# Sparse attention into a routed mixture of experts: routing and constants issued in pieces, a shorter tile list, half weight loads, expert units placed anew, and output scaling on ACT

## The chip, the cores and the metric

One core of a Trainium2 chip runs the whole program. The metric is the device time of one execution in microseconds (us), which is the span from the first to the last instruction plus 1.6 to 2.1 us. Timings came from several chips, numbered in the runs. Every comparison is made on one chip, or names the chips.

Engines: PE is TensorE, PEld its weight loads, DVE is VectorE, ACT is ScalarE, POOL is GpSimd, SP is SyncE.

## The reference, cut to what matters

```python
# B, H, S, D = 4, 8, 768, 64; block, window = 32, 16;  N, DM, E, F = 3072, 512, 8, 1024
k_sum = k.reshape(B, H, nb, block, D).max(axis=3)
v_sum = v.reshape(B, H, nb, block, D).mean(axis=3)
scores = concat(where(|i - j| < window, q k / 8, -1e9), q k_sum / 8 + log(block))
attn = softmax(scores) @ concat(v, v_sum)
x = attn.transpose(0, 2, 1, 3).reshape(N, DM)

logits = x @ w_gate + modality_bias[modality_id]      # 8 experts, one per token
e_idx, gate = argmax(logits), softmax(logits)[e_idx]
out[mask_e] = gate * (relu(x[mask_e] @ w1[e]) @ w2[e])
```

## The kernel before

The kernel runs attention in 16 **steps**, one for each batch and pair of heads. Behind every fourth step a batch is complete and is **routed**: logits, one-hot, the place of each token in its expert's region of a DRAM buffer `xs`, six indirect DMAs of 128 rows that **scatter** the tokens there, and the **tile list**, which says which expert tiles (256 tokens of one expert) are now full. A tile's rows then come back as `xr`, are transposed (`px`), and go through w1, ReLU and w2. An expert tile is cut into **units** (a `yield` each, one group of eight matmuls), and the table `UNITS` says how many of them each attention step carries. TensorE takes its matmuls in program order, so where a unit is placed decides what stands behind it.

What the change touches (cut):

```python
    def later_constants():                 # one block, at the end of step 0
        nc.vector.tensor_scalar(erev, cidx[:, 0:E], -1.0, float(E), op0=ALU.mult, op1=ALU.add)
        # ... eleven more small DVE operations ...
        for t in xrs:                      # 8 row buffers
            nc.gpsimd.memset(t, 0.0)
        # ... eight more, then
        pm = bank([128, NJ], FP16, "pm")
        nc.tensor.transpose(pm, mh, ident[0:NJ, 0:NJ])
        nc.vector.tensor_copy(midf, pm)

    # in expert_tile:
            nc.vector.tensor_scalar_mul(ot, po, gt)

    UNITS = [0] * 6 + [3] * 4 + [6] * 4 + [0, 0]

    def weights_ahead(n):                  # guessed experts' weights, 1 MB each
        when = {1: (0, 0), 2: (0, 1), 4: (1, 0), 5: (1, 1)}
        if n in when:
            u, w = when[n]
            # ... expert index from the guess ...
            load_weights(u, gv[u], which=(w,))

    for n in range(np_):
        u = [UNITS[n] * (i + 1) // 6 - UNITS[n] * i // 6 for i in range(6)]
        # load(n + 5)
        weights_ahead(n)
        scores(n, 1)
        if new and cc == 1:
            enlist(*new)                   # rows and weights of the new tiles
        if n and cc == 0:
            features(n - 1)
            router = route(b - 1)
            step(router)                   # logits to one-hot, in one go
        pump(u[0])
        # keys(n + 2); pump(u[1])
        values(n, 0)
        # summaries(n + 2)
        if router:
            step(router)                   # ranks, index, six scatters
        # pump(u[2]); queries(n + 2); pump(u[3]); blocks(n + 1); scores(n + 1, 0)
        if router:
            drain(router)                  # the tile list, some 30 DVE operations
        # pump(u[4]); features; values(n, 1)
        if n == 0:
            later_constants()
        pump(u[5])
```

The softmax here doesn't subtract the row's maximum and nothing guards it: scores larger than these inputs give would overflow.

## Time and profile before

| | kernel before |
|---|---|
| timed, first pair (4 runs) | 276.9 us (276.3 to 277.7) |
| profiled execution | 269.1 us, span 267.5 |
| busy: PE, DVE, ACT, POOL | 189.3, 161.6, 105.2, 128.1 us |
| DVE instructions | 486 |

The profiled execution is 7.5 us shorter than the timed ones. The page's rows of 40 equal slices (busy share of PE in tenths, then the TensorE clock that was granted) show the holes of the first half and the half clock that follows each:

```profile
PE   1272088693436979849999799597870998999920
PEclk9999559759555797985999889889596899999975
```

Counted from 0, a slice being 6.7 us, slices 3 and 4 are the constants' hole, 10 to 12 step 6, and 28 to 30 the last routing. The prediction shows the lines of these holes.

### The profile page before, as it was taken

How to read it: one execution, taken by the hardware profiler on the slowest of the kernel's cores; microseconds unless marked ns; L12 is line 12 of the kernel's file. 1: busy time of each engine (PE TensorE's matmuls, PEld its weight loads, DVE VectorE, ACT ScalarE, POOL GpSimd, SP SyncE). 2: the span in 40 equal slices, each digit the busy share in tenths (PEclk: the TensorE clock that was granted, in tenths of full speed). 3: DMA queues.
4: the chain of work that ended last, by engine and by line, in shares of the span. 5: the costliest groups of instructions: out<-in, count | busy, mean ns of one | idle time of the engine just before them, and what ended most of it. 6: DMA issues, size and time to landing. Idle time of an engine off the chain costs nothing. (4 is left out here: it accounts for less than half of the span.)

```text
span 267.5 us, 6780 instructions
## 1 busy us (share of the span) xinstructions
PE 189.3 (71%) x2680; PEld 133.9 (50%) x2680; DVE 161.6 (60%) x486; ACT 105.2 (39%) x185; POOL 128.1 (48%) x202
## 2 busy tenths in 40 slices
PE   1272088693436979849999799597870998999920
PEld 0162077583334756723768465375550674677600
DVE  2539969988923675998566668957659224232110
ACT  2256069566303643831548145354030321333300
POOL 7739948727606432587305046530155776422220
PEclk9999559759555797985999889889596899999975
DMA  6996099996794961139802012330022333211100
GB/s 87 190 171 92 1 170 207 207 208 163 116 222 63 144 88 45 41 121 220 195 2 82 0 59 82 98 125 0 21 100 79 83 79 157 82 78 78 76 16 0
DMA packets 20027, 27.09 MB, mean 101 GB/s; under 512 B 2812, under 2 KB 16404, under 8 KB 19988
## 3 DMA queue, kind: packets, MB, share of 16 engines
q0 software_dynamic: 17360, 24.17, 43.9%
q1 hardware_dynamic: 2628, 2.41, 3.2%
q8 instruction: 23, 0.38, 0.6%
q14 instruction: 16, 0.13, 0.2%
HBM read 85.27 MB, written 10.25 MB: 357 GB/s over the span
## 5 line engine op out<-in xcount | busy, mean ns | idle before, releaser
L515 PE MATMUL pmo<-w2b,hT 128*128 128x512 f16 x208 | 57.6, 432 | 7.6 <-DVE tk L445 7.6
L504 PE MATMUL ph<-xg,w1b 128*128 128x256 f16 x416 | 53.8, 283 | 4.6 <-DVE at L490 3.3
L521 POOL DMA_INDIRECT out_dram<-ot,at x26 | 25.8, 992 | 57.8 <-DVE ot L520 44.0
L507 ACT ACTIVATE hT<-ph 128x512 f16<-128x512 f32 x52 | 31.1, 608 | 48.8 <-PE ph L504 48.8
L504 PEld LDWEIGHTS <-w1b 128*128 128x128 f16 x416 | 39.9, 101 | 13.3 <-issue 3.7
L250 ACT ACTIVATE pT<-pss 128x384 f16<-128x384 f32 x64 | 28.1, 505 | 44.0 <-PE pss L246 43.4
L515 PEld LDWEIGHTS <-hT 128*128 128x128 f16 x208 | 21.5, 108 | 33.5 <-issue 17.6
L520 DVE TENSOR_SCALAR ot<-pmo,xr 128x512 f32<-128x512 f32 x26 | 19.3, 747 | 29.1 <-PE pmo L515 22.0
L251 DVE TENSOR_TENSOR pT<-pT,bmask 96x768 f16<-96x768 f16 x32 | 19.2, 599 | 18.9 <-ACT pT L250 18.9
L201 ACT COPY kv<-pk 128x768 f16<-128x768 f16 x32 | 24.2, 808 | 15.9 <-PE pk L200 15.9
L358 POOL DMA_INDIRECT xs<-xb,posi x24 | 24.1, 1003 | 11.6 <-issue 5.8
L224 ACT COPY qT<-pq 128x768 f16<-128x768 f16 x16 | 13.0, 812 | 17.8 <-PE pq L222 17.8
L204 POOL COPY kv<-kv 128x352 f16<-128x352 f16 x16 | 7.9, 494 | 23.3 <-ACT kv L201 23.2
L233 PE MATMUL pv<-ident,kv 128*128 128x128 f16 x192 | 16.5, 248 | 3.1 <-POOL kv L214 3.1
L272 DVE TENSOR_TENSOR xb<-po,rec 128x384 f16<-128x384 f32 x32 | 17.8, 558 | 1.2
L281 PE MATMUL pt<-ident,xb 128*128 128x128 f16 x96 | 10.1, 240 | 11.6 <-DVE xb L272 11.6
L488 DVE COPY xg<-px 128x1024 f16<-128x1024 f16 x13 | 8.9, 685 | 15.4 <-PE px L486 15.4
L246 PE MATMUL pss<-qT,kv 64*128 64x64 f16 x384 | 12.7, 205 | 5.7 <-POOL kv L214 5.5
L233 PEld LDWEIGHTS <-kv 128*128 128x128 f16 x192 | 14.0, 112 | 4.5 <-POOL kv L214 3.7
L211 DVE TENSOR_REDUCE ks<-kv 128x24 f16<-128x768 f16 x16 | 15.1, 943 | 1.1 <-ACT kv L201 1.1
L214 POOL COPY kv<-ks 128x576 f16<-128x576 f16 x16 | 10.7, 669 | 10.1 <-DVE ks L213 9.4
L234 ACT COPY vb<-pv 120x768 f16<-120x768 f16 x16 | 13.1, 818 | 5.4 <-PE pv L233 5.4
(142 smaller groups left out, 300.8 us busy)
## 6 DMA issues: line engine op xcount, KB each, us to landing
w1b<-in_moe_w_dram POOLq DMA_DIRECT2D x15, 1024.0 KB
w2b<-in_moe_w_dram POOLq DMA_DIRECT2D x15, 1024.0 KB
kn<-in_k_dram POOLq DMA_DIRECT2D x16, 192.0 KB
vn<-in_v_dram POOLq DMA_DIRECT2D x16, 192.0 KB
qn<-in_q_dram POOLq DMA_DIRECT2D x16, 192.0 KB
xr<-xs SPq DMA_DIRECT2D x8, 258.0 KB, 5.9
out_dram<-ot,at POOLq DMA_INDIRECT x26
xs<-xb,posi POOLq DMA_INDIRECT x24
```

What stands on the lines that cost most here:

```text
L201: nc.scalar.copy(kv[:, i, :, 0:64].rearrange("p t (s c) -> p t s c", c=C8), bass.AP(pk.tensor, pk.offset, [pk.ap[0], [8, NT], [1, 8], [P8, ...
L211: nc.vector.reduce_max(ks[:, 0], kv[:, 0, :, 0:64].rearrange("p t (g s) -> p t g s", g=2), axis=AX.X)
L233: nc.tensor.transpose(pv[:, tl, :], kv[:, 1, 6 * half + tl, :], ident)
L250: nc.scalar.activation(pT[:, h], pss[h], AF.Exp, scale=SCALE)
L251: nc.vector.tensor_tensor(pT[0:WK], pT[0:WK], bmask[0:WK, None, 6 * half:6 * half + 6, :].to_broadcast([WK, 2, 6, 64]), op=ALU.mult)
L272: nc.vector.tensor_tensor(xo, po[:, :, :, 0:D], rec.unsqueeze(3).to_broadcast([128, 2, 3, D]), op=ALU.mult)
L358: apart("xs", nc.gpsimd.indirect_dma_start(out=xs[:, :], out_offset=bass.IndirectOffsetOnAxis(ap=posi[:, c:c + 1], axis=0), in_=xb[:, c, : ...
L504: nc.tensor.matmul(ph[:, f, :], w1[:, c, ts(2 * f2 + f, 128)], xg[:, c, :], start=(c == 0), stop=(c == NCD - 1))
L507: nc.scalar.activation(hT[:, 2 * f2:2 * f2 + 2, :], ph, AF.Relu)
L515: nc.tensor.matmul(po, hT[:, f, ts(s2, 128)], w2[:, f, :], start=(f == 0), stop=(f == NF - 1))
L520: nc.vector.tensor_scalar_mul(ot, po, gt)
L521: apart("out", nc.gpsimd.indirect_dma_start(out=out[:, :], out_offset=bass.IndirectOffsetOnAxis(ap=at[:, s2:s2 + 1], axis=0), in_=ot[:], i ...
```

## The change

Its intent: no DVE block may stand in front of attention. The constants shrink; fourteen small ones move in front of the first step, and the rest come in pieces; routing is a generator of fifteen pieces, one `tick()` each between attention's parts; the tile list takes about half the operations; the guessed weights are loaded in halves, one per step (two in step 2), behind GpSimd's neighbour copies; units are placed by a string for each step; and ACT scales the output. The diff, cut to its core:

```diff
@@ constants
-        for t in xrs:
-            nc.gpsimd.memset(t, 0.0)
+        for t in xrs[-2:]:
+            nc.vector.memset(t, 0.0)
+        yield                               # and seven more yields between the rest
@@ routing: a yield behind every two or three operations; fused operations
-        nc.vector.tensor_scalar(can, lg, 0.0, None, op0=ALU.is_ge)
-        nc.vector.tensor_tensor(can, can, bc(erev, NC), op=ALU.mult)
+        st_(can, lg, 0.0, bc(erev, NC), op0=ALU.is_ge, op1=ALU.mult)
+        yield
@@ tile list: one selection over a table in place of counting and indexing
+        nc.vector.tensor_tensor_scan(cu, v2, v2, 0.0, op0=ALU.add, op1=ALU.bypass)
+        nc.vector.tensor_tensor(sel, bc(v2, T), bc(cidx[:, 1:T + 1], K * E, 2), op=ALU.is_equal)
+        nc.vector.tensor_tensor(pd, sel..., tab..., op=ALU.mult)
+        nc.vector.reduce_sum(lf[:, 0:T, 0:3], pd, axis=AX.X)
@@ expert_tile
-            nc.vector.tensor_scalar_mul(ot, po, gt)
+            nc.scalar.activation(ot, po, AF.Copy, scale=gt)
@@ schedule
-    UNITS = [0] * 6 + [3] * 4 + [6] * 4 + [0, 0]
+    UNITS = {6: "000011", 7: "101010", 8: "101110", 9: "101010",
+             10: "000111", 11: "111110", 12: "101110", 13: "101110", 14: "101110", 15: "101110"}
@@ weights_ahead
-        when = {1: (0, 0), 2: (0, 1), 4: (1, 0), 5: (1, 1)}
+        for p in {1: (0,), 2: (1, 2), 3: (3,), 4: (4,), 5: (5,), 6: (6,), 7: (7,)}.get(n, ()):
+            load_weights(p // 4, gv[p // 4], which=(p // 2 % 2,), part=p % 2)
@@ loop: tick() between all parts; enlist(...) at the end of each second step of a batch
```

## The prediction

> **What bounds the kernel now.** I read the page first, then a table of nine stretches, then the list of PE in order of time, and last the waits of the stretches with holes. The page gives PE 189.3 us of a 267.5 us span, so no engine is full on average, and the question is which engine is missing where. The stretches (columns: span, then busy of PE, weight loads, DVE, ACT, POOL; granted clock, DMA share, GB/s) are cut at PE's holes and at borders of loop steps:
>
> ```profile
> 0.00:15.00 15.00, 2.60 (x50) 2.04 (x52) 5.58 (x30) 3.68 (x4) 11.87 (x25) 1.00 0.95 146
> 22.50:34.50 12.00, 0.06 (x5) 0.01 (x1) 11.61 (x25) 1.74 (x4) 11.78 (x16) 0.63 0.47 53
> 34.50:69.20 34.70, 25.48 (x604) 21.81 (x606) 30.45 (x98) 23.18 (x41) 21.26 (x33) 0.75 1.03 190
> 69.20:89.00 19.80, 10.69 (x140) 7.96 (x138) 10.39 (x20) 5.30 (x9) 8.55 (x18) 0.50 0.88 141
> 89.00:122.70 33.70, 27.93 (x455) 19.05 (x454) 25.80 (x89) 17.50 (x32) 17.16 (x27) 0.85 0.44 90
> 122.70:187.60 64.90, 57.16 (x825) 37.93 (x824) 45.00 (x129) 30.45 (x56) 21.95 (x37) 0.89 0.30 82
> 187.60:206.80 19.20, 11.02 (x99) 7.65 (x100) 13.39 (x61) 2.63 (x5) 8.23 (x10) 0.77 0.19 70
> 206.80:257.60 50.80, 47.49 (x336) 31.36 (x335) 14.76 (x30) 14.33 (x24) 24.32 (x34) 0.97 0.24 85
> ```
>
> Row two is an almost dead PE. Row three (loop steps 1 to 5) is bound by DVE, 30.45 of 34.7 us. Row four is step 6, with both engines half idle. Rows five and six are near PE's bound with holes in each routing. Row seven is the last routing, row eight the remaining expert tiles, which fill PE. The holes, from PE's list in order of time:
>
> ```profile
> 34.49 0.20 PE L181 MATMUL pm<-ident,mh 24*128 24x24 f16 x1 [11.94 <-DVE mh L179]
> 68.24 0.50 PE L281 MATMUL pt<-ident,xb 128*128 128x128 f16 x3 [4.74 <-DVE xb L272]
> 77.69 1.04 PE L486 MATMUL px<-ident,xr 128*128 128x128 f16 x8 [6.59 <-DMA xr<-xs]
> 84.17 1.46 PE L233 MATMUL pv<-ident,kv 128*128 128x128 f16 x12 [2.52 <-POOL kv L214]
> 118.26 0.50 PE L281 MATMUL pt<-ident,xb 128*128 128x128 f16 x3 [3.42 <-DVE xb L272]
> 170.92 1.03 PE L504 MATMUL ph<-xg,w1b 128*128 128x256 f16 x8 [3.34 <-DVE at L490]
> ```
>
> The first is the block of constants, the second, fifth and sixth are the tile-list arithmetic (some 30 dependent DVE operations in one run) standing in front of attention's DVE work. The third and fourth come with the Pool's wait for its own weight load; the whole waits have it beside the last hole, where PE stands until the last tile list is in a register:
>
> ```profile
> POOL w2b L187 <- DMA w2b<-in_moe_w_dram: 11.1, 1, 11.1
> ...
> PE pmo L515 <- DVE tk L445: 7.6, 1, 7.6
> ```
>
> Why the constants take so long is in the lines by form: three DVE operations on 8 or 16 elements stand for 6 us each, exactly under the Pool's eight memsets.
>
> ```profile
> L169 POOL MEMSET xr<- 128x1032 f16 x8 | 7.3, 974 | 0.0
> L153 DVE TENSOR_SCALAR erev<-cidx 128x8 f32<-128x8 f32 x1 | 6.2, 6205 | 0.0
> ```
>
> **What the Trainium skill says.** (1) "SBUF — State Buffer", section "Who interferes with whom": DVE in a two-port mode and GpSimd share one port pair by an exclusive lock, and the loser fully blocks. The trace agrees: erev, an fp32 tensor_scalar, lasts 6205 ns until the memsets end, while equal small ones elsewhere last 0.16 to 0.29 us. (2) "TensorE: Matmul & The Clock Gate", Part 1: after an idle window of about 3.4 us PE runs at half clock. The trace agrees: eight w2 matmuls take 1.89 us warm and 3.55 us at 124.6, after the hole at 118. So a hole costs more than its length. (3) "ScalarE: Activation LUTs", "What ACT_TABLE_LOAD costs": 186 ns + 0.833 N with immediate scale, 93 ns more with a pointer scale. For N=512 that is 612 ns; the trace's ReLU is 608 (31.1 us in 52), so the new scaling is estimated at 0.70 us, DVE's being 0.747. (4) "DMA: Bandwidth & Descriptors", "Bandwidth": 1 MB takes 6.15 us alone. Here the last guessed load (issued 70.33, waited for until 82.41) took some 12 us, behind q, k, v and row loads. So halves issued earlier should wait far less.
>
> **The change part by part.**
>
> *Start, +1 us.* Load 1 now goes ahead of the iotas: three Pool issues, 0.63 us apart, move them 1.9 us. The mask constants' end moves from 8.7 to 10.6; early constants (14 small operations) add 1.9; two summary reductions (0.86 + 0.94) and the Pool copy (0.67) give first scores at 15.1 against 14.96. The Pool is no longer behind load issues, but DVE takes that place. Load 3 then stands before summaries 1, worth up to 1 us. No gain here.
>
> *Constants, -5.4 us.* PE's hole is 12.0, but DVE finishes step 0's work at 25.6, so only 25.6 to 34.2 is lost, 8.6. What is left as pieces: two memsets of 0.5, and about ten operations, 3.2 in all, still on the bound engine. 8.6 - 3.2 = 5.4.
>
> *Routing 0 and its list in the DVE-bound stretch, -4.2.* Before: eight operations to one-hot at about 0.22 (1.75), nine to the scatter (1.9), about thirty from cf to done (6.1), two tk (0.5): 10.2. After: eleven at 0.22 (2.5) plus sixteen at 0.2 (3.3): 6.0. A normal step's DVE work is, start to start, 2x0.48 mask, 2x0.21 reciprocal, 2x0.47 scale, 2x0.86 reductions, 0.47 vb, 0.48 xT: 5.0 us; steps 1 to 3 took 5.1 on average, so savings here shorten the span one for one. Step 6 should start at 69.2 - (5.4 + 4.2 - 1) = about 60.5.
>
> *Step 6, -8.3.* Before 19.8 with 3 expert units. The weight wait goes; tile 1's weights come at step 7, where the Pool waits for half a megabyte, an estimate of 4 to 5 us, with neighbour copies already out and two steps of slack. What stays: six scatters at 1.29 each (7.7), then the row load of about 6 to 7, against a first expert unit placed five stations into the step. From the scatters' start to rows is some 15.7 us, PE arrives 2 to 4 earlier. 5.5 attention + 2 units at 1.2 + 3.5 wait = 11.5.
>
> *Steps 7 to 15, -12.6.* Before 98.6 with 33 units. A clean step is step 11 (137.48 less 148.96): 11.48 us, PE full, 6 units. Six units cost about 7.3 (eight w1 matmuls four times 0.93, px 0.5, w2 twice 1.82, less overlap), so a unit is 1.22 and attention 4.1. After, 34 units: 34x1.22 = 41.5; attention 7x4.1 + 2.6 + 1.8 = 33.1; routing matmuls 1.6: 76.2. To this I add DVE in step 9 (5.0 + 0.4 + list 4.0 = 9.4 against PE's 7.8) 1.6, rows of list 1 about 2 and the half clock behind it 2, Pool at step 7 1, rest 3: 86. Spreading 8 units into steps 14 and 15, which had none, fills their 0.5 us holes.
>
> *Last routing and tail, -6.* The units left are 43 both times (36 of 79 done), and PE does them at 7.39 us per six in the last stretch. The last list is not shorter: before, cf to li is 6.97; after, two operations on 1440 elements (estimated 1.65 each, from 0.66 for 480) eat what the fewer operations save, and I sum to 7.0. But pr and pc matmuls no longer stand behind blocks of three units (pr waited 3.8, pc 3.5). Chain from pl: 1.9 to one-hot, 2.1 through pr to the scatter index and count, 1.3 through pc, 7.0: 12.3, beside eight units of 9.9. Hole 2.5 to 3.5 instead of 7.6, and less half clock (two stretches of eight w2 matmuls at 3.2 and 3.4 instead of 1.9): -6.
>
> Scaling on ACT is worth nothing alone: DVE loses 26x0.747 = 19.3 us where PE is the bound.
>
> Sum: -4.2 + 1 - 5.4 - 8.3 - 12.6 - 6 = -35.5 of the span. Taken off the timed run: 276.6 - 35.5 = 241.
>
> **The rivals.**
> *DMA takes over.* The stretch at 34.5 already has a DMA share of 1.03 at 190 GB/s. Without the hole, loads and half-weights come closer together: 3.7 MB in about 16 us of steps 1 to 3, 230 GB/s, above what it moved. For it: the numbers. Against: q, k, v are five steps ahead, and only one wait for kn shows, at the start. If it binds, half of the constants' and step 6's gain goes: 248.
> *The new wait on ACT.* With three ot buffers, scaling waits for the out scatter behind ten gathers; DVE waited 6.6 us for it at 216.9 and PE lost 1.25. On ACT the ReLUs stand behind it. I expect some 1 us, at most 4: 242 to 245.
> *DVE stays the bound.* If the shorter list's pieces each wait for PE or the wider operations run slower, steps 8, 9, 12, 13 keep 1.5 each: 247.
> *Everything overlaps well*: no row waits, holes closed in step 6: 232.
>
> **Range and chances.** Two thirds of the gain are closed holes that one can point at; one third is my assumption of 92% PE efficiency after step 6. If I get only half of steps 6 to 15, it is 251; if rows never wait, 232. 241, range 229 to 255. Faster by over 2% (under 271) 0.95, within 2% 0.04, slower 0.01.
>
> **What would show it.** Right: no PE hole over 4 us between 20 and 140; the small constants at 0.2 us; step 6 starting near 60; the end of attention near 158; the last hole 2 to 4 us; the Pool's longest weight wait under 6. Wrong: waits of PE for kn or vn (DMA), of hT behind ot on ACT, or PE in the middle stretch under 85% busy. A rise in slower matmuls at full occupancy would break my unit price.

## The result, and the profile after

Ratios here are the mean time of one kernel's fast runs over that of the other's fast runs of the same rounds, so not quite the ratio of the medians that are quoted. Executions over 1.5% slower than the fastest of the same kernel are left out of the means.

| first pair | before | after |
|---|---|---|
| timed, 4 runs each | 276.9 us | 268.2 us (266.3 to 270.6) |
| ratio | | 0.966 (0.960 to 0.972) |
| span of the profiled run | 267.5 | 266.6 |
| busy PE, DVE, ACT, POOL | 189.3, 161.6, 105.2, 128.1 | 193.5, 128.1, 122.4, 126.3 |
| DVE instructions | 486 | 361 |

The change is faster by 3.4%. The predicted 241 us and its range, 229 to 255, are missed by far. The page's same two rows for the changed kernel:

```profile
PE   0375966753859895597998776998973829999920
PEclk9999996555558999577999995999999965999995
```

The first 30 us are fuller than before, but there are weak slices where I had foretold none: 9 (60 to 67 us), 15 and 16 (100 to 113), 30 and 32 (200 to 207 and 213 to 220). What TensorE does there is in its list in order of time (start, duration, line, operation, then the idle time before it and what ended it), here in step 9:

```profile
104.95 0.28 PE L287 MATMUL po<-vb,pT 120*64 120x65 f16 x5 [0.50 <-issue]
105.71 0.26 PE L287 MATMUL po<-vb,pT 120*64 120x65 f16 x4 [0.49 <-issue]
106.45 0.21 PE L287 MATMUL po<-vb,pT 120*64 120x65 f16 x1 [0.48 <-issue]
...
108.62 1.01 PE L498 MATMUL ph<-xg,w1b 128*128 128x256 f16 x4 [0.45 <-issue]
...
112.25 0.24 PE L244 MATMUL pq<-ident,qn 96*64 96x96 f16 x1 [0.36 <-issue]
```

Twelve `po` matmuls, ordinarily one group of 0.36 us, are cut into **bursts** that start some 0.72 to 0.76 us apart. "issue" means that TensorE waited for nothing that the profile shows. The other engines wait for TensorE meanwhile, and the releaser is not even seen. That is how the page's group of the ReLU reads in this run, and below it the same group in the rerun that follows:

```profile
L501 ACT ACTIVATE hT<-ph 128x512 f16<-128x512 f32 x52 | 30.6, 605 | 20.3 <-remote 13.9
L501 ACT ACTIVATE hT<-ph 128x512 f16<-128x512 f32 x52 | 31.0, 603 | 9.1 <-PE ph L498 6.9
```

There are four such stretches (59.5 to 66, 104 to 113, 156 to 163, and parts of 197 to 220 us), and each lies in a row of GpSimd's indirect DMAs: three rows of six scatters, and the last routing's scatters with ten gathers behind them. Many records of semaphores are missing too: counted in the stored trace (no page shows the count), there are 2,710 records of semaphore updates.

So there are two questions. What are the bursts? And what did the change do apart from them?

### The profile page after: what moved, and what is told of

Read it like the earlier page. It is cut to its first block, busy times and chain, and to the rows that moved or that the text cites. A ratio compares the mean times of both kernels' runs of the same rounds, so it can differ in the third digit from the quotient of the medians.

```text
span 266.6 us, 6691 instructions
## 1 busy us (share of the span) xinstructions
PE 193.5 (73%) x2684; PEld 137.1 (51%) x2684; DVE 128.1 (48%) x361; ACT 122.4 (46%) x211; POOL 126.3 (47%) x198
## 5 line engine op out<-in xcount | busy, mean ns | idle before, releaser
L509 PE MATMUL pmo<-w2b,hT 128*128 128x512 f16 x208 | 53.4, 407 | 6.1 <-issue 4.2
L498 PE MATMUL ph<-xg,w1b 128*128 128x256 f16 x416 | 54.7, 283 | 3.6 <-issue 3.6
L509 PEld LDWEIGHTS <-hT 128*128 128x128 f16 x208 | 20.2, 102 | 30.7 <-issue 8.5
L514 ACT ACTIVATE ot<-pmo,xr 128x512 f32<-128x512 f32 x26 | 18.0, 692 | 28.9 <-PE pmo L509 26.2
L290 DVE RECIPROCAL rec<-po 128x6 f32<-128x6 f32 x32 | 6.0, 187 | 30.6 <-PE pq L244 13.2
L255 PE MATMUL pv<-ident,kv 128*128 128x128 f16 x192 | 18.8, 268 | 1.8 <-POOL kv L236 1.0
L287 PE MATMUL po<-vb,pT 120*64 120x65 f16 x384 | 15.3, 215 | 6.5 <-issue 2.9
L244 PE MATMUL pq<-ident,qn 96*64 96x96 f16 x256 | 13.5, 244 | 7.2 <-issue 6.3
L255 PEld LDWEIGHTS <-kv 128*128 128x128 f16 x192 | 15.8, 123 | 5.2 <-issue 2.2
L268 PE MATMUL pss<-qT,kv 64*128 64x64 f16 x384 | 13.3, 211 | 5.9 <-POOL kv L236 5.9
```

The costliest lines, as they stand in the source:

```text
L255: nc.tensor.transpose(pv[:, tl, :], kv[:, 1, 6 * half + tl, :], ident)
L287: nc.tensor.matmul(po[64 * (tl % 2):64 * (tl % 2) + 64, h, tl // 2, :], pT[0:KR, h, tl, :], vb[0:KR, 6 * half + tl, h, :])
L498: nc.tensor.matmul(ph[:, f, :], w1[:, c, ts(2 * f2 + f, 128)], xg[:, c, :], start=(c == 0), stop=(c == NCD - 1))
L509: nc.tensor.matmul(po, hT[:, f, ts(s2, 128)], w2[:, f, :], start=(f == 0), stop=(f == NF - 1))
L514: nc.scalar.activation(ot, po, AF.Copy, scale=gt)
```

## The experiments

### Is it the kernel? (both kernels once more, on chip 3)

No edit.

> The changed kernel once more, unedited. In its first trace TensorE runs four stretches (59.5-66.2, 103.7-113.0, 155.9-163 and parts of 197-220 us) in bursts of five to ten instructions about 0.72 us apart, with no wait that the profile shows, some 20 us of loss by my reading; each lies in a run of GpSimd's indirect DMAs. If this is a property of the kernel's order (theory A: the runs of indirect DMAs; theory B: a place in TensorE's own instruction stream), all four come back within 2 us of those times, and the time is 266 to 271. If it is chance, they move or vanish and the time falls below 262.

> The kernel before once more, because its first trace (267.5 us) is 8 us shorter than its timed runs (276 to 278). If the timed runs of the kernel before hold the same bursts of TensorE in some runs of indirect DMAs, this trace will be about 275 long and show gaps of 0.7 us without a shown wait, 5 to 10 us in sum, and then theory A covers both kernels. If it shows none, and is again near 268, the state of the clock alone made the difference.

Measured, one run each, so of unknown state: changed kernel **242.7** us, before 263.3 (span 261.7). The kernel before took 261.3 to 268.9 in seven further runs there. All the bursts are gone, and there are 3,263 records of updates in place of 2,710 for the same program. The expectation "all four come back" was wrong: the bursts are not in the kernel's order alone. Two of the four rows of indirect DMAs, as stretches (span; then busy time with the count of instructions of PE, PEld, DVE, ACT, POOL; clock; DMA share; GB/s). First the first trace of the changed kernel:

```profile
104.10:111.50 7.40, 3.93 (x26) 1.66 (x25) 0.41 (x2) 0.80 (x1) 5.87 (x6) 0.64 0.35 129
202.10:217.60 15.50, 8.82 (x63) 5.42 (x64) 0.76 (x2) 3.38 (x6) 12.22 (x16) 0.93 0.30 85
```

Then the same rows of DMAs in the rerun on chip 3:

```profile
98.00:105.40 7.40, 6.64 (x146) 4.67 (x143) 7.13 (x22) 5.75 (x12) 5.88 (x8) 1.00 0.38 136
184.60:200.10 15.50, 12.03 (x76) 6.96 (x74) 1.52 (x4) 4.45 (x7) 12.14 (x16) 0.89 0.35 102
```

GpSimd takes the same 5.9 us for its scatters both times and the DMA share is about the same, but TensorE gets 26 matmuls through instead of 146. The two stretches don't begin at the same matmul, so here is the same piece of work, from the first `po` to the last `pq` of step 9. It took 9.3 us in the first trace (104.24 to 113.50) and 1.8 us in the rerun, where these lines are its first and last. At half clock throughout it would be some 3.6 us, so the clock alone does not explain it:

```profile
97.45 0.36 PE L287 MATMUL po<-vb,pT 120*64 120x65 f16 x12
...
98.72 0.53 PE L244 MATMUL pq<-ident,qn 96*64 96x96 f16 x16
```

### Two kinds of chips (the changed kernel on whatever chip came)

No edit in the four anchors.

> The changed kernel unedited, timed against the kernel before on the chip of these runs. On chip 3 one look gave 242.7 against 264.7, in the first pair of timings 268.2 against 276.9. If the bursts of TensorE belong to the chip or to its state in the first pair, they show here only if both kernels are again near 268 and 277; otherwise a ratio of 0.91 to 0.92 and 241 to 245 us.

> The changed kernel unedited, as the anchor of these runs: ratio 0.91 to 0.92 to the kernel before on a chip that runs that in 262 to 266. If the chip is one that runs the kernel before in 276 to 278, the bursts of TensorE are expected again, at 59-66, 104-113, 156-163 and 197-220 us, and 266 to 271 us.

> The changed kernel unedited as the anchor: 241 to 245 with 3,260 to 3,280 records of semaphore updates on a chip that runs the kernel before in 262 to 266; 266 to 271 with bursts and some 2,700 records of updates on a chip that runs it in 276 to 278. A chip of the second kind has to show both together, or my tie between them is wrong.

> The changed kernel unedited once more, for another chip. 239 to 245, some 3,270 records of semaphore updates and no bursts where the kernel before takes 262 to 267; 266 to 271, some 2,700 records and bursts at 59-66, 104-113, 156-163 and 197-220 us where it takes 276 to 278. The two have to go together if the first pair's chip or state is the cause.

| chip | before, us | after, us | records of updates, after | bursts |
|---|---|---|---|---|
| first pair (not numbered) | 276.9 | 268.2 | 2,710 | yes |
| 3 | 264.7 | 242.7 | 3,263 | no |
| 14 | 263.9 | 242.3 and 242.6 fast, 246.7 and 246.8 slow | 3,277 | no |
| 1 | 265.2 | 242.9 | 3,268 | no |
| 6 | 266.5 | 239.8 | 3,273 | no |
| 2 | 276.1 | 266.9 and 270.2 | 2,757 | yes |

The tie held: slower kernel before, bursts, and missing records come together. On the common kind the change gives 0.916 (0.909 to 0.923; chip 1) and 0.897 (0.888 to 0.906; chip 6); on the other kind 0.97. So few draws of chips hardly say how common each kind is, and only chip 6 was drawn in two rounds (the common kind both times), so that the chip itself makes the kind is likely and not shown.

### Do the bursts need a row of indirect DMAs? (spread scatters; and the kernel before on such a chip)

```diff
-        for c in range(NC):
-            apart("xs", nc.gpsimd.indirect_dma_start(...))   # six in a row
+            for _ in take(b, cf, TAKE[b], i0, TAKE[b]):      # batches 0 to 2
+                if left:
+                    scatter(left.popleft())                  # one behind each piece
+                yield
```

> The changed kernel with the six scatters of batches 0 to 2 issued one behind each piece of the tile list in place of six in a row. If the chip is one of the kind of the first pair (kernel before at 276 to 278, changed kernel at 266 to 271 with TensorE's bursts inside each run of scatters), theory A expects the bursts of steps 5, 9 and 13 to go and 10 to 14 us with them; a rival (chip or profiler state that slows TensorE whatever GpSimd does) expects them to stay. If the chip is of the kind of chips 1, 3 and 14, neither has bursts: GpSimd's neighbour copies no longer stand behind six scatters (7.7 us), but the rows come later; 0 to 3 us either way (240 to 246).

> The kernel before, for a trace of it on a chip of the kind of chip 22 (where it takes 276 and the changed kernel 267 to 270), if one comes up. If bursts of TensorE inside GpSimd's indirect DMAs explain its 12 us too, its trace shows them in one or more of its runs of scatters and gathers, 10 to 14 us in sum, with fewer records of semaphore updates than the 3,313 of chip 3. On a chip of the common kind: 262 to 266 and none.

> The changed kernel with spread scatters, again for a chip of the kind of chip 22. On the common kind it takes 250 to 255. Theory A (TensorE falls into bursts only beside a run of indirect DMAs): the bursts of steps 5, 9 and 13 go and it takes 255 to 262, less than the changed kernel's 267 to 270 there. Rival (the chip slows TensorE near indirect DMAs, in a row or not): bursts are spread over the same 24 scatters and it takes 270 to 280. On a chip of the common kind: 250 to 255 and none.

(Where these texts write "chip 22", chip 2 is meant.)

On chip 6, of the common kind, spreading is **worse**: 250.1 to 255.2 us against the anchor's 239.8, where I had expected 240 to 246. The rows come later, and TensorE stands at them. The waits of that run (engine, tile, line, releaser; us in total, times, longest) say it:

```profile
PE px L488 <- DMA xr<-xs: 20.9, 2, 11.4
```

The two runs came to chip 13, of the other kind. The kernel before took 274.0, and its trace has the bursts too, in its second and third row of scatters, with 2,766 records of updates where chip 3 had 3,313:

```profile
111.37 0.29 PE L265 MATMUL po<-vb,pT 120*64 120x65 f16 x5 [0.49 <-issue]
...
114.27 0.24 PE L222 MATMUL pq<-ident,qn 96*64 96x96 f16 x1 [0.44 <-issue]
```

The kernel with spread scatters took 269.5 there, not the 255 to 262 that I expected of theory A. But where the time went supports that theory in part. In step 5, where the changed kernel has bursts on such chips from 59.5 on, TensorE's list is now whole:

```profile
60.21 0.83 PE L244 MATMUL pq<-ident,qn 96*64 96x96 f16 x16
60.98 1.46 PE L255 MATMUL pv<-ident,kv 128*128 128x128 f16 x12
```

Counted by TensorE's list: from the common kind to the other, the end of attention moves by 15.5 us with rows of six (166.4 on chip 3, 181.9 on chip 2) and by 5.4 with spread scatters (178.8 on chip 6, in a trace marked slow, and 184.2 on chip 13). The part from there to TensorE's last matmul, whose scatters and gathers I did not spread, grows by about 9 both times (63.0 to 71.7, and 63.0 to 72.1). So on these chips bursts come beside indirect DMAs in a row, and mostly go when there is room between them. It does not pay, because a row of six has the rows back sooner than spread scatters do.

Why does the change suffer twice as much as the kernel before (26 us against 12)? A likely reason, not tested: the bursts cost only where TensorE has work. In the kernel before, the first row of scatters lies beside the tile list, when TensorE waits for DVE in any case. What the bursts are is **not settled**. The missing records may have the same cause, and nothing here tells a slow TensorE from a congested one. Instruction fetches show no difference: the pages give the two instruction queues 23 and 15 packets in both traces, and 0.7 and 0.9% of the DMA engines' time. That the recording of a run takes part is not excluded either, since each run here, timed or profiled, has a recorded span and clock.

### Where the rest of the gain is missing (chips of the common kind)

From here on all is on chips without bursts. The two traces from chip 3, by the start of the second half of the scores of each step (from TensorE's list in order of time), with my predicted terms:

| stretch | before | after | difference | predicted |
|---|---|---|---|---|
| start to step 6 | 68.7 | 63.6 | -5.0 | -8.6 |
| step 6 | 19.7 | 11.5 | -8.2 | -8.3 |
| step 7 to the end of attention | 91.9 | 91.3 | -0.5 | -12.6 |
| from there to the end | 81.5 | 74.5 | -7.0 | -6 |
| span | 261.7 | 240.9 | -20.8 | -35.5 |

Steps 7 to 15 gave nothing. In the changed kernel's list on chip 3, one hole leaps out:

```profile
113.55 1.03 PE L479 MATMUL px<-ident,xr 128*128 128x128 f16 x8 [8.02 <-DMA xr<-xs]
114.37 3.53 PE L509 MATMUL pmo<-w2b,hT 128*128 128x512 f16 x8
```

TensorE stands 8 us in step 10 at the transposes of the second list's first tile, until its rows land, and then runs eight w2 matmuls at half clock in 3.53 us (warm: 1.89). This hole is 8.02, 6.24, 8.05 and 4.70 us in the four traces of the changed kernel on such chips (3, 14, 1, 6); in the rerun of the kernel before, TensorE does not wait at these rows. Before it, GpSimd had waited for the second guessed tile's weights, its longest wait, ahead of the neighbour copies of step 8 and so of that batch's scatters (98.0 to 105.4). That this wait is what makes the rows late was not tested alone:

```profile
90.77 0.04 POOL L209 DMA_DIRECT2D w2b<-in_moe_w_dram  x1 [8.42 <-DMA w2b<-in_moe_w_dram]
```

**Units behind the rows.** Attention of steps 10 and 11 is ready to run in that hole, but stands behind the transposes. The Trainium skill says why ("TensorE: Matmul & The Clock Gate", Part 2, step 1): the matmuls "stay in program order", and only weight loads are pulled ahead. The trace agrees: in these 8.02 us TensorE runs nothing. So I moved the units, 36 as before:

```diff
-             10: "000111", 11: "111110", 12: "101110", 13: "101110", 14: "101110", 15: "101110"}
+             11: "000011", 12: "101110", 13: "111111", 14: "111111", 15: "111111"}
```

> The changed kernel with the same 36 expert units between attention, but none in step 10 and the first two of the second list at the end of step 11. In the rerun of the changed kernel TensorE stands 8.02 us (from 105.5 to 113.55) at the transposes of tile 2 until the rows xr land, and then runs eight w2 matmuls in 3.53 us where they take 1.89 warm; my prediction gave the rows of the second list 2 us and the half clock 2. If the loss is the order of TensorE's own instructions (attention of steps 10 and 11 stands behind the transposes), these two steps fill the wait and the time falls by 6 to 9 us against the changed kernel on the same chip (about 234 to 237 where that is 242.7). Rival: the later steps then lack TensorE time or DVE takes over as the bound (5.0 us a step), and the time stays within 2 us.

> The version with the units placed behind the rows (none in step 10, two at the end of step 11) once more, on whatever chip comes. On a chip of the common kind (before 262 to 267): 234 to 237, ratio 0.89 to 0.90. On a chip of the kind of chips 2 and 13 (before 274 to 278): 258 to 264, still below the changed kernel's 267 to 270 there, because attention of steps 10 and 11 then lies in the stretch in which TensorE is slowed.

Measured on chip 14: **236.1** us (235.7 to 237.8), against 242.3 and 242.6 of the changed kernel's fast runs there; ratio to before 0.897 (0.891 to 0.902). On chip 6 again, 238.1 (234.7 to 238.8), 0.901 (0.883 to 0.920); there the changed kernel's two runs, in other rounds, were 238.9 and 240.7, so the gain is smaller (2.8 us by fast means) and less certain there; the hole to be filled was smaller too, 4.70 us. The hole at the rows is gone, the transposes run when they are reached, and w2 is warm:

```profile
115.42 0.62 PE L479 MATMUL px<-ident,xr 128*128 128x128 f16 x8
115.88 1.89 PE L509 MATMUL pmo<-w2b,hT 128*128 128x512 f16 x8
```

That is 6 us on chip 14 by placing alone, as expected. It beats both kernels on the common kind; on the other kind it was not run.

**The old placing.**

```diff
+    UNITS = {n: "010101" if n < 10 else "111111" for n in range(6, 14)}
```

> The changed kernel with the kernel before's placing of its 36 expert units (three in each of steps 6 to 9, six in each of steps 10 to 13, none in 14 and 15); all else changed. Whole weight loads cost only 0 to 2 us, so the weights do not explain that step 6 fell from 19.7 to 11.5 us. Theory: the placing does, because TensorE no longer stands at the transposes of rows that have not landed while attention waits behind them. Then step 6 is again 18 to 20 us, and the time is 8 to 11 us above the changed kernel (ratio to before 0.95 to 0.96 in place of 0.92). Rival: the shorter list and its pieces bring the rows earlier, and the placing is worth under 3 us (ratio 0.92 to 0.93).

> The kernel before with the changed kernel's placing of expert units and nothing else. If the placing is worth 8 to 11 us by itself: 253 to 256 where the kernel before is 264 (ratio 0.955 to 0.97). If it needs the other parts (rows earlier, list in pieces): 260 to 266.

Measured on chip 1: the changed kernel with the old placing 250.5 (248.6 to 256.3, ratio 0.943), the anchor 242.9. The new placing is worth 7 us in this kernel (fast means 249.8 and 242.7), a little under the 8 to 11 that I expected. Step 6 is then 15.1 us, not 18 to 20. TensorE stands at both lists' rows:

```profile
70.41 1.03 PE L479 MATMUL px<-ident,xr 128*128 128x128 f16 x8 [7.36 <-DMA xr<-xs]
...
114.78 1.03 PE L479 MATMUL px<-ident,xr 128*128 128x128 f16 x8 [7.07 <-DMA xr<-xs]
```

In the kernel before, the new placing by itself gives 261.3 where that kernel is 265.2, ratio 0.989 (0.980 to 0.998): 3 us. My reading, which no run isolates: the placing is worth more where less DVE work stands in front of the attention that it lets through.

**The weights whole.** The loads of the kernel before, whole and at the head of steps 1, 2, 4 and 5, in the changed kernel.

> The changed kernel with the weight loads of the kernel before: whole (1 MB), one each at the head of steps 1, 2, 4 and 5. My prediction gave step 6 a gain of 8.3 us, most of it from this part, and the step did come out at 11.5 us in the rerun. So by the prediction: 5 to 8 us slower than the changed kernel on the same chip, with a wait of GpSimd for the weights of 9 to 12 us in step 6. Rival: GpSimd waits 8.4 us for half a weight load at step 8 in the rerun (w2b, 82.35 to 90.77), so the halves only move the wait two steps on; then the time is within 2 us, or better.

Measured on chip 14: 245.0 (242.9 to 246.2), 2 us above the anchor's fast runs. The halves help step 6 (16.0 us without them, 11.5 to 13.1 in the four traces with them). The hole at the second list's rows is this without them:

```profile
114.70 1.03 PE L479 MATMUL px<-ident,xr 128*128 128x128 f16 x8 [4.57 <-DMA xr<-xs]
```

With halves it was 4.70 to 8.05 us, so one trace does not show that it shrank because of the loads. In the two traces of this chip (14), the kernel with whole loads starts step 7 2.7 us later (79.1 against 76.4) and ends attention 2.4 us later (168.4 against 166.0): what the halves gain in step 6 stays. It is smaller than the 5 to 8 us that the prediction gave, and the rival's "within 2 us" is just missed.

**The constants in a block**, with all eight memsets on GpSimd again.

```diff
-    side.append(later_constants())
+        if n == 0:
+            drain(later_constants())
-        for t in xrs[-2:]:
-            nc.vector.memset(t, 0.0)
+        for t in xrs:
+            nc.gpsimd.memset(t, 0.0)
```

> The changed kernel with the later constants in one block at the end of step 0 and all eight row buffers cleared on GpSimd again. Prediction: 5.4 us slower than the changed kernel (the hole of TensorE before step 1 returns, to 30 to 34 us in place of 26.6, with DVE operations of several us under the memsets). Rival: the loads of q, k and v and the weight loads bind the next stretch (DMA share 1.19 at 190 GB/s from 26.5 to 47), so a later start is made good there: 0 to 2 us slower.

Measured on chip 14: 249.9 (248.3 to 253.0); fast runs mean 249.4 against 242.5, so 6.9 us, a little above the predicted 5.4; what the block and what the memsets cost is not told apart. DVE's list shows small operations standing under the memsets again, and TensorE's what waits for them:

```profile
26.93 8.16 DVE L178 COPY prow<-pidx 128x1 f32<-128x1 f32 x1
```

```profile
35.85 0.20 PE L192 MATMUL pm<-ident,mh 24*128 24x24 f16 x1 [10.74 <-DVE mh L188]
```

**A longer list.** Fourteen dependent operations of 8 elements in front of every list:

```diff
+        for _ in range(14):
+            nc.vector.tensor_scalar_add(cf, cf, 0.0)
```

> The changed kernel with 14 small dependent DVE operations (8 elements each, about 0.2 us) put in front of every tile list, so that the lists are about as long in operations as those before. By my prediction each of the three lists in attention that is shorter shortens the span, and the last one too: 2.8 us each, 7 to 11 us in all. Rival: lists 0 to 2 lie beside the scatters and the rows' landing, which set when an expert tile can start, and only the last one stands in TensorE's way: 2 to 4 us.

Measured on chip 1: 253.7 (250.8 to 255.2) against 242.9, and 10 us by the means of the fast runs: near the top of what the prediction gives. The padding is one block of 3.5 us for the first list, so this run tests length and block together. TensorE waits for attention's mask behind it, and at the end for the list:

```profile
70.55 0.55 PE L287 MATMUL po<-vb,pT 120*64 120x65 f16 x12 [6.40 <-DVE pT L273]
...
193.54 2.38 PE L500 MATMUL ph<-xg,w1b 128*128 128x256 f16 x16 [4.12 <-DVE li L441]
```

**Routing in three blocks** at the places of the kernel before, list as short as after.

```diff
+    def fine():                        # replaces every tick() of the loop
+        if n < 4:
+            tick()
@@ behind features, first step of a batch
+            tick(4)
@@ behind summaries
+        if n > 3:
+            tick(4)
@@ behind scores(n + 1, 0)
+        if n > 3:
+            tick(99)
```

> The changed kernel with its routing of batches 0 to 2 issued in three blocks at the three places where the kernel before has them (the constants stay in short pieces). By my prediction the short pieces save little beyond the shorter list: the blocks cost TensorE one hole of 3 to 4 us each in three steps, 270 to 278. If the bursts come from the scatters lying beside full TensorE work (theory A), the blocks put TensorE to rest on DVE's pieces ahead of the scatters but leave the scatters in a row of six, and the bursts stay, about as long. If they vanish, theory A in its plain form is wrong, because the scatters are still there: then it is what lies beside them.

Measured on chip 3: 240.9 and 241.7 fast, 244.8 and 248.2 slow. I expected 270 to 278 and was wrong twice: the base was that of the other kind of chip, and the blocks cost nothing on balance: step 8 takes 17.4 us in place of 14.0, and TensorE then doesn't wait at the second list's rows. With the short list, pieces are worth no more than three blocks. The pieces have a price of their own: the matmuls of the ranks and counts stand in TensorE's order while the DVE pieces that they need stand behind attention's (before `oh`, two summary reductions of 0.94 us each). In the changed kernel on chip 3:

```profile
54.79 0.20 PE L354 MATMUL pr<-oh,upper 128*128 128x48 f16 x1 [2.54 <-DVE oh L347]
...
58.01 0.17 PE L379 MATMUL pc<-tot,ones 128*128 128x8 f16 x1 [2.00 <-DVE tot L372]
```

**Scaling back on DVE.**

```diff
-            nc.scalar.activation(ot, po, AF.Copy, scale=gt)
+            nc.vector.tensor_scalar_mul(ot, po, gt)
```

> The changed kernel with the scaling of the output back on DVE. My prediction said 0 us for this part; the rival (ACT's new wait) says that the ReLU waits in ACT behind the scaling: the ReLU groups show 20.3 us of idle before them, 13.9 of it 'remote'. Rival: 262 to 265, 3 to 6 us faster than the changed kernel. Prediction: within 2 us of it (266 to 271), and the bursts stay.

Measured on chip 3: 243.4, 245.5 and 245.5 fast (249.8 slow), where one run of the changed kernel took 242.7. It is not faster, so ACT's new wait costs nothing that shows; whether ACT gains a microsecond or two is not settled by one run of the anchor. The numbers that I had written, 262 to 271, were again those of the other kind of chip.

## Why the prediction was wrong, by its own steps

- **The base.** "Taken off the timed run: 276.6 - 35.5 = 241." The trace that I took the steps from was 7.5 us shorter than those timed runs. It had none of the bursts and 3,327 records of updates, like the traces of the common kind, while 276 to 278 is what the kernel before takes on the other kind. I took a difference found in one kind off a time from the other. That the rerun came to 242.7 us is chance: on the common kind my own steps give 264 - 35.5, about 228, and it took 242.6.
- **Steps 7 to 15, -12.6: this step failed.** Measured -0.5. Three terms in it were wrong. (a) "rows of list 1 about 2 and the half clock behind it 2": measured 8.0 (4.7 to 8.05 in four traces) and 1.6 (3.53 less 1.89). Moving the units took back 6 us on chip 14, 2.8 on chip 6. (b) The before side, 98.6 us, came from an execution marked slow; by the same cut to the end of attention, it was 97.1 in that trace and 91.9 in the rerun, so 5 us of my gain was never there. (c) About 1 us is left over.
- **"92% PE efficiency after step 6."** For steps 7 to 15 my own terms give 76.2 of 86, 89%. On the common kind TensorE was busy 77.1 of the 91.3 us after step 6, 84%, which is below the 85% that I had named as a sign of being wrong; with the units moved it was 74.7 of 82.9, 90%. On the chips of the first pair's kind the assumption fails outright: in the rows of indirect DMAs TensorE was busy 3.9 of 7.4 us, and 8.8 of 15.5. Nothing in the profile of before pointed at it, as that execution had no bursts. It explains the other half of the miss of 27 us: the changed kernel loses 26 us there (span 266.6 against 240.9), the kernel before 12 to 13 (276.6 against 264), and the difference, 13, comes on top of the 14.7 by which my terms were too large.
- **Routing 0 and its list, -4.2.** (The terms for after add up to 5.8, not 6.0.) Measured about 0: from the second half of the step 4 transposes to step 6 it is 16.6 us in both kernels on chip 3. The list is shorter, but pieces and TensorE now wait for each other in turn (2.54 and 2.00 us above). The padded list costs 10 us, but there length and block come together.
- **Constants, -5.4, and start, +1.** Right. TensorE's hole was 2.2 us at `pm` in place of 11.9, and at the start of step 4 the changed kernel was 5 us ahead (42.8 against 48.1); putting the block back costs 6.9. (The three DVE operations that "stand for 6 us each" start within 0.15 us and end together, so that was one stall of 6.2 us.)
- **Step 6, -8.3.** Measured -8.2, with 11.5 us as foretold, though three other traces of the changed kernel have 12.6 to 13.1. Two reasons are shown, each by two traces of one chip: the halves (2.9 us: 16.0 without them, 13.1 with) and the placing of the units (2.2 us: 15.1 with the old one, 12.8 with the new). The rest stays open.
- **Last routing and tail, -6.** Measured -7.0. The holes left there are 1.36 us at the list and 2.39 and 1.08 at the gathered rows, 4.8 in all, more than the 2.5 to 3.5 foretold, in place of one hole of 7.8; one set of eight w2 matmuls still runs at half clock there, two did before:

```profile
181.56 1.91 PE L498 MATMUL ph<-xg,w1b 128*128 128x256 f16 x16 [1.36 <-DVE li L439]
...
187.58 0.23 PE L479 MATMUL px<-ident,xr 128*128 128x128 f16 x1 [2.39 <-DMA xr<-xs,gi]
```

- **Scaling on ACT, 0.** Right within what can be told. The operation takes 0.692 us, estimated at 0.70.
- **The signs I named.** Step 6 near 60: 63.6. End of attention near 158: 166.4, and 159.2 once the units are moved. No hole over 4 us between 20 and 140: wrong (8.02). GpSimd's longest weight wait under 6: wrong (8.42).
- **The rivals.** None of mine explains the miss. DMA did not bind TensorE in the middle: it never waits there for `kn` or `vn`. The wait behind `ot` on ACT shows once, 1.1 us in step 8. Of the third, pieces that each wait for PE did show, but in step 4 (2.54 and 2.00 us) and hardly in the steps that it named (1.3 at most).

## What to carry to other kernels

Before taking a difference off a time, check that the trace and the timed runs belong together. A trace several per cent shorter than the runs, or one marked slow, is another base, and another chip can be too. Where TensorE takes its work in order, the place of the first instruction that needs a far-away result (here the rows that come back through DRAM) can be worth as much as the work itself: 6 to 7 us for a line of digits on two chips, some 3 on a third. And a gain can turn into a wait at the next far-away result: the kernel before did not wait for the second list's rows in its rerun, the faster one stood there for 4.7 to 8.05 us. So measure a part by undoing it alone, in more than one trace.

## What the Trainium skill lacked or had wrong

- "DMA: Bandwidth & Descriptors" and "TensorE: Matmul & The Clock Gate" don't have it: on some chips TensorE falls into bursts 0.72 to 0.76 us apart beside a row of GpSimd's indirect DMAs, at a granted clock of 0.64 in one stretch and 0.93 in another (9.3 us for work that otherwise took 1.8), and the same program takes 267 to 270 us in place of 240 to 243. The mechanism is open.
- I found no page on two chips that time one kernel so differently: the same kernel took 274 to 278 us in every run on some and 261 to 271 on others.
- "Perfetto Trace Analysis" has no sign to tell such an execution (other pages speak of lost records in general, not as a sign of this): here it was the count of records of semaphore updates, 2,710 and 2,757 for the changed kernel in place of 3,263 to 3,277.
- "TensorE: Matmul & The Clock Gate", Part 1, gives an idle window of about 3.4 us before the half clock. After the 8.02 us hole it was borne out (eight w2 matmuls in 3.53 us in place of 1.89), but in three traces a hole of only 2.02 to 2.31 us was enough: before `pv` of step 1, `pq` ran at full clock (0.51 us), and `pv` behind the hole took 1.46 us in place of 0.84. In a fourth, a hole of 2.45 us there was not.
